# Query and key weights in two halves on two DMA queues, with a new order of instructions

## The chip, the core and the metric

The kernel runs on one core of a Trainium2 chip. The core has five engines with their own instruction queues: TensorE (PE in the profile) does matrix products into PSUM, VectorE (DVE) and ScalarE (ACT) do elementwise work and copy results out of PSUM, GpSimd (POOL) does small work in SBUF, and SyncE (SP) starts transfers between the chip's main memory and SBUF. Sixteen DMA engines carry these transfers, whichever engine started them. Engines wait for each other by semaphores, and each works through its queue in order, so that an instruction that waits holds up everything behind it. The metric is device time in microseconds (us) of one execution; lower is better.

## What is computed

One sequence of 2048 tokens of 448 features, all in bfloat16, goes through an attention block and a mixing block, each with a layer norm before it and a residual after it. The attention has 16 heads of 28 features. Each token attends to eight tokens, itself and those 2, 4, ... 14 positions before it.

```python
h  = x + A(layernorm(x), wqkv, wo)
h2 = h + B(layernorm(h), w_in, w_sp, b_sp, w_out)

# A: q, k, v = x @ wqkv, in 16 heads of 28
idx    = pos[:, None] - 2 * arange(8)[None, :]
logits = einsum('bhsd,bhswd->bhsw', q, k[idx]) * 28 ** -0.5     # masked where idx < 0
o      = einsum('bhsw,bhswd->bhsd', softmax(logits), v[idx])
A      = o @ wo

# B
z      = gelu(x @ w_in)                # 1792 features
z1, z2 = z[:896], layernorm(z[896:])
g      = einsum('ts,bsf->btf', w_sp, z2) + b_sp
B      = (z1 * g) @ w_out
```

## The kernel before

Everything stays in SBUF between the first load and the last store. The tokens are cut into 16 blocks of 128. For each block the kernel computes the mean and variance of x (DVE, lines 677 and 679), the reciprocal root of the variance (POOL, lines 671 and 672), and the normalised block xn (DVE, line 688). The products need xn with features on the partitions, which is called xhT. The first four blocks are transposed on PE by a product with the identity (lines 716 and 719) and copied out of PSUM by the helper `move` (line 576). The other twelve are transposed by DMA.

The weights of q and k are loaded into `wraw`, and DVE and ACT copy them into `wqk`, where each head is padded from 28 to 32 rows. There are eight of these copies, `wp0_0` to `wp3_1`: group g (four heads) and k = 0 for q or 1 for k. A product needs the copies of its own group alone. The products of q and k (`product`, line 565) run over six token ranges `QT`, of which the first two have 128 tokens each. For each range there are four groups, each with eight matmuls into two PSUM banks: six with all 128 rows (features 0 to 383) and two with 64 rows (features 384 to 447), which sit in the upper and lower half of the array. `move` copies the result into `qkT`. Then follow, in 18 pieces of about 112 queries, the logits (line 842, 16 small matmuls), exp (ACT, line 851), the mask (DVE, line 857), the product with v (line 866), the division, a DMA transpose, the product with wo, the residual and the second layer norm. The mixing block follows: w_in, gelu, the second norm, the large product with w_sp (line 1004), the gate (lines 1013 and 1016), the product with w_out (line 1028), the last residual (line 1035) and the stores.

The order is not that of the source. Every piece of work is a `Job` for one engine with the tiles that it reads and writes. `Planner.order` lists the jobs with an assumed duration each, and picks for every engine the ready job that can start, with the lowest rank from the table `PRIO`; `LOOK` says how far ahead an engine may wait for a better-ranked job. `ON` moves single copies to another engine. PSUM banks are tickets that a job takes and another one gives back. The resulting order is then issued with the semaphore waits that the tiles demand. Several names matter below:

- `FIRST` is the order of the first loads, all on SP's queue: x of block 0, the weights of q and k, x of block 1, x of blocks 2 and 3, and so on. The ranks decide the real order among them.
- The job `tbl` on ACT loads the table for exp and runs a small activation that writes two elements of the tile `warm`.
- The filler job, also called warm, is a matmul on constant data that PE does while it has nothing else, until the time `WARMT`. It keeps PE busy at the start. `COLD` is the time until which the planner counts it double.
- `load_c` loads a matrix of 448 rows as one transfer of 384 rows (three to a partition) and two of the last 64 rows, once for each half of the array.

Of the kernel before, what the change touches and what calls it, by code (L numbers as in the profile page):

```python
# [5 lines left out]
S_TOK = 2048  # L6
D = 448
# [5 lines left out]
NB = 16  # L13
# [11 lines left out]
LOOK = {'pe': 0.06465927487231404, 'act': 0.07391855863952959, 'dve': 0.1969035871511503, 'pool': 0.02318129821447599,  # L25
        'sp': 0.10267676699206288}
PRIO = [1, 2, 4, 3, 0, 5, 10, 9, 7, 6, 8, 13, 33, 11, 12, 34, 47, 40, 41, 45, 18, 15, 71, 0, 0, 17, 13, 12, 13, 24, 14,
        23, 27, 22, 25, 28, 26, 0, 3, 11, 14, 16, 7, 8, 11, 9, 6, 15, 3, 16, 12, 1, 16, 5, 18, 29, 17, 12, 17, 20, 17, 23, 15,
        19, 23, 26, 2, 22, 21, 25, 5, 29, 10, 22, 24, 4, 23, 38, 9, 29, 45, 11, 32, 27, 36, 32, 48, 28, 31, 30, 34, 8, 52, 7,
        24, 43, 6, 25, 63, 57, 26, 44, 1, 20, 58, 42, 39, 55, 49, 35, 47, 50, 20, 56, 66, 38, 65, 2, 35, 67, 83, 31, 61, 3, 37,  # L30
        18, 10, 10, 4, 0, 22, 1, 0, 8, 4, 20, 20, 18, 2, 18, 21, 14, 4, 22, 11, 19, 23, 19, 15, 1, 3, 13, 0, 13, 21, 15, 9, 12,
        34, 28, 8, 29, 30, 53, 5, 6, 2, 39, 41, 16, 59, 56, 36, 58, 54, 38, 50, 52, 37, 46, 53, 54, 69, 76, 78, 63, 57, 88, 62,
        71, 42, 42, 51, 89, 102, 96, 109, 92, 95, 56, 91, 103, 65, 89, 86, 48, 24, 27, 7, 10, 24, 35, 6, 46, 49, 51, 40, 21, 30,
        32, 9, 7, 5, 37, 25, 41, 33, 19, 39, 43, 31, 14, 47, 27, 38, 26, 64, 33, 62, 81, 87, 36, 77, 80, 94, 100, 93, 101, 105,
        32, 99, 126, 77, 103, 98, 14, 40, 30, 48, 39, 60, 37, 82, 59, 68, 48, 44, 26, 25, 61, 41, 45, 28, 84, 55, 75, 74, 73,
        27, 83, 85, 104, 122, 116, 107, 96, 33, 69, 34, 75, 97, 31, 19, 64, 40, 36, 43, 86, 81, 85, 79, 72, 43, 70, 67, 34, 60,
        31, 68, 46, 77, 72, 80, 76, 30, 44, 107, 94, 125, 70, 123, 115, 133, 44, 117, 39, 76, 119, 41, 69, 66, 32, 74, 33, 95,
        90, 91, 102, 36, 17, 79, 75, 44, 73, 35, 78, 50, 90, 93, 71, 128, 37, 16, 117, 111, 129, 121, 138, 130, 113, 40, 135,
        110, 82, 162, 43, 85, 88, 29, 87, 47, 92, 104, 131, 127, 35, 73, 84, 82, 49, 65, 45, 97, 67, 114, 110, 118, 132, 38, 74,
        98, 55, 100, 57, 108, 99, 124, 134, 106, 70, 149, 125, 134, 137, 156, 155, 167, 182, 49, 146, 47, 55, 141, 42, 52, 101,  # L40
        105, 60, 116, 63, 133, 64, 147, 129, 136, 153, 46, 54, 77, 118, 53, 108, 66, 112, 139, 145, 154, 45, 49, 171, 152, 143,
        139, 197, 172, 191, 195, 63, 193, 59, 62, 198, 60, 61, 109, 106, 58, 131, 54, 120, 52, 111, 146, 166, 150, 168, 53, 95,
        112, 62, 113, 59, 148, 141, 144, 179, 50, 56, 174, 165, 168, 220, 228, 231, 236, 233, 55, 248, 56, 79, 251, 58, 80, 114,
        115, 120, 122, 76, 127, 78, 151, 136, 170, 142, 48, 63, 241, 121, 70, 147, 72, 176, 153, 192, 199, 61, 64, 107, 206,
# [33 lines left out]
WLH = [4, 4, 8, 9, 18, 1, 4, 12, 24, 4, 14, 34, 6, 22, 21, 26]  # L78
GRES = 1
WARMT = 9.0  # L80
COLD = 7.2
FIRST = [(0, 1), "q", (1, 2), (2, 4), "v", (4, 8), (8, 12), (12, 16), "o"]
LN1G = [(0, 1), (1, 1), (2, 2), (4, 4), (8, 4), (12, 4)]
QT = [(0, 128), (128, 256), (256, 512), (512, 1024), (1024, 1536), (1536, 2048)]
# [120 lines left out]
class Planner:  # L205
# [9 lines left out]
    def job(self, name, eng, key, ops, dur, lat=None, acq=None, rel=None, use=(), after=(), reserve=0, tbl=None, srv=None, kind="F", peer=None):  # L215
        j = Job()
# [884 lines left out]
```

## Time and profile before

| | us |
|---|---|
| median of 3 runs | 244.10 |
| lowest and highest | 244.07, 245.21 |
| the profiled execution's own time | 244.28 |
| its span, first to last instruction | 242.5 |
| PE busy in the span | 234.5 |
| DVE busy | 153.5 |
| ACT busy | 92.3 |
| POOL busy | 40.0 |
| start of the first product with wqk | 8.78 |
| start of the first exp | 14.58 |

The busy time of an engine is a mean over stages with different limits: DVE is close to full until about 110 us and far from it later, and PE is close to full from about 9 us to the end. Matmuls are pipelined, so a matmul's duration in the profile contains its latency; the pace is read from the time that a row of them takes. Times in the text are counted from the start of the span.

### The profile page before, as it was taken

To read this page: it belongs to the slowest core of one execution; us is meant where nothing else is said; L and a number is where in the kernel's file an instruction comes from. 1 tells how busy PE (TensorE), PEld (TensorE's weight loads), DVE (VectorE), ACT (ScalarE), POOL (GpSimd) and SP (SyncE) were. 2 spreads that over 40 slices of the span, in tenths; PEclk is the share of its full clock that TensorE was granted. 3 is DMA by queue.
4 is the path that set the end of the run, shared out by engine and by line. 5 is a ranking of instruction groups with operands and counts; after the bars stand their busy time and mean duration, and the time that the engine had idled before them with its cause. 6 is when DMAs were issued, how large, how long until landed. Compare 5 with 4: busy or idle time off the path is not lost.

```text
span 242.5 us, 4316 instructions
## 1 busy us (share of the span) xinstructions
PE 234.5 (97%) x1735; PEld 114.1 (47%) x1755; DVE 153.5 (63%) x328; ACT 92.3 (38%) x114; POOL 40.0 (16%) x96
## 2 busy tenths in 40 slices
PE   5799999999999999999999999999999999999995
PEld 3565445454545444434444444444444454444453
DVE  4799988999889899999753302602305194416263
ACT  2698768747796998963341000000000000011000
POOL 8346210123232402343111000000000000000000
PEclk9999999999999999999999999999999999999999
DMA  6945565697557878694699950000000002011002
GB/s 186 323 122 103 97 119 120 147 143 178 111 110 105 151 111 171 150 173 118 127 191 167 194 103 0 3 0 0 0 3 1 0 0 78 19 38 38 19 21 95
DMA packets 66468, 23.23 MB, mean 96 GB/s; under 512 B 58896, under 2 KB 66192, under 8 KB 66448
## 3 DMA queue, kind: packets, MB, share of 16 engines
q1 hardware_dynamic: 66448, 22.95, 45.5%
q8 instruction: 14, 0.23, 0.4%
q14 instruction: 6, 0.05, 0.1%
HBM read 6.83 MB, written 1.84 MB: 36 GB/s over the span
## 4 chain that ended last, share of the span: by engine, by line
PE 93%; DMA 2%; DVE 2%; issue 1%; SPq 1%; DVEq 0%
PE psum L1004 40%; PE psum L565 38%; PE psum L1028 9%; PE psum L866 3%; PE psum L842 3%; DMA wraw<-in_A_wqkv_dram 2%; DVE st L677 1%; SPq L591 1%; DVE wqk L576 0%; PE psum L716 0%; DVE srg L1035 0%; DVE xn L688 0%; PE psum L719 0%; DVE mv L679 0%; DVEq L183 0%
## 5 line engine op out<-in xcount | busy, mean ns | idle before, releaser
L1013 DVE TENSOR_TENSOR ub<-psum,bb 128x512 bf16<-128x512 f32 x28 | 19.3, 691 | 53.1 <-PE psum L1004 52.2
L1004 PE MATMUL psum<-wsp_hi,z2p 128*128 128x512 bf16 x220 | 50.6, 379 | 0.2
L971 ACT ACTIVATE z1p<-psum 128x1024 bf16<-128x1024 f32 x14 | 14.0, 1021 | 94.1 <-PE psum L565 94.1
L851 ACT ACTIVATE E<-psum 128x896 bf16<-128x896 f32 (+2 forms) x36 | 31.8, 929 | 8.0 <-PE psum L842 8.0
L1004 PEld LDWEIGHTS psum<-wsp_hi,z2p 128*128 128x128 bf16 x224 | 21.8, 98 | 26.3 <-issue 0.4
L565 PE MATMUL psum<-xhT,wqk 128*128 128x512 bf16 (+5 forms) x186 | 27.8, 306 | 1.8 <-DVE wqk L576 1.2
L1004 PE MATMUL psum<-wsp_la,z2p 128*128 128x512 bf16 x108 | 26.1, 379 | 0.2
L1004 PE MATMUL psum<-wsp_lb,z2p 128*128 128x512 bf16 x110 | 26.0, 379 | 0.1
L565 PE MATMUL psum<-w_in,hnT 128*128 128x448 bf16 (+1 forms) x128 | 25.2, 353 | 0.0
L565 PE MATMUL psum<-hnT,w_in 128*128 128x512 bf16 (+1 forms) x108 | 23.0, 379 | 0.4 <-issue 0.3
L1028 PE MATMUL psum<-w_out,z1p 128*128 128x448 bf16 (+1 forms) x119 | 22.5, 341 | 0.0
L930 DVE BATCH_NORM_STATS2 st<-z2p 128x6 f32<-128x448 bf16 x32 | 19.2, 615 | 4.0 <-ACT z2p L926 3.5
L857 DVE TENSOR_TENSOR E<-E,maskb 128x1792 bf16<-128x1792 bf16 (+2 forms) x18 | 19.6, 1100 | 1.3 <-ACT E L851 1.2
L677 DVE BATCH_NORM_STATS2 st<-x_tm 128x6 f32<-128x448 bf16 x32 | 19.1, 609 | 1.6 <-DMA x_tm<-in_A_x_dram 1.4
L565 PEld LDWEIGHTS psum<-xhT,wqk 128*128 128x128 bf16 (+1 forms) x192 | 13.0, 96 | 12.0 <-issue 2.3
L672 POOL TENSOR_TENSOR rs<-rs,negh 128x2 f32<-128x2 f32 (+2 forms) x22 | 17.6, 801 | 1.8
L1035 DVE TENSOR_TENSOR srg<-psum,x_tm 128x448 bf16<-128x448 f32 (+1 forms) x17 | 10.0, 593 | 11.4 <-PE psum L1028 9.6
L1004 PEld LDWEIGHTS psum<-wsp_lb,z2p 128*128 128x128 bf16 x112 | 10.9, 98 | 13.3 <-issue 0.4
L1004 PEld LDWEIGHTS psum<-wsp_la,z2p 128*128 128x128 bf16 x112 | 11.0, 98 | 13.1
L1028 PEld LDWEIGHTS psum<-w_out,z1p 128*128 128x128 bf16 x119 | 11.6, 98 | 10.2
L565 PEld LDWEIGHTS psum<-w_in,hnT 128*128 128x128 bf16 (+1 forms) x128 | 9.8, 97 | 12.3 <-issue 4.2
L565 PEld LDWEIGHTS psum<-hnT,w_in 128*128 128x128 bf16 (+1 forms) x112 | 9.1, 97 | 11.9 <-issue 2.5
(58 smaller groups left out, 233.9 us busy)
## 6 DMA issues: line engine op xcount, KB each, us to landing
w_in<-in_B_w_in_dram SPq DMA_DIRECT2D x8, 224.0 KB, 3.7
out_dram<-srg SPq DMA_DIRECT2D x16, 112.0 KB, 1.7
x_tm<-in_A_x_dram SPq DMA_DIRECT2D x3, 448.0 KB, 5.9
w_out<-in_B_w_out_dram SPq DMA_DIRECT2D x1, 784.0 KB, 5.3
wraw<-in_A_wqkv_dram SPq DMA_DIRECT2D x1, 672.0 KB, 4.8
bb<-in_B_b_sp_dram SPq DMA_DIRECT2D x1, 512.0 KB, 5.5
wv<-in_A_wqkv_dram SPq DMA_DIRECT2D x1, 336.0 KB, 6.4
wo<-in_A_wo_dram SPq DMA_DIRECT2D x1, 336.0 KB, 6.0
```

Of the source, the lines that this page charges most:

```text
L565: ins = e.matmul(o, w, x, start=g not in seen, stop=left[g] == 0, **kw)
L672: (lambda e: e.tensor_tensor(R, A, negh[:, 0:1].to_broadcast([128, n]), ALU.pow), [rr, r_negh], r_rs[k][m:m + n])],
L677: [(lambda e: e.bn_stats(st[:, m, :], src), [rsrc], [r_st[k][m]])], dve_t(D))
L842: ins = e.matmul(psum[:, c:c + nq], qkT[p:p + DH, 2 * g + 1, k0:k0 + NK], qkT[p:p + DH, 2 * g, t0:t0 + nq], start=True, stop=True, tile_po ...
L851: return e.activation(o, i, AF.Exp, scale=SCALE)
L857: return e.tensor_tensor(a, a, maskb[:, 0:1, pad:pad + nq].to_broadcast([NK, NHEAD, nq]), ALU.mult)
L930: [(lambda e, m=m, k=k: e.bn_stats(st3[:, m, k, :], z2p[:, m, D * k:D * (k + 1)]), [r_z2[m]], [r_st[2][m]])], dve_t(D))
L971: return e.activation(o, i, AF.Gelu_apprx_tanh)
L1004: ins = e.matmul(psv(tk), z2p[:, s, 128 * fc:128 * fc + 128], w[:, 512 * (tc % 2):512 * (tc % 2) + 512], start=(s == 0), stop=(s == NB - 1))
L1013: [(lambda e, tc=tc, s=s, tk=tk: e.tensor_tensor(ub[:, s, :], psv(tk), bb[:, 512 * tc:512 * tc + 512], ALU.add), [r_bb], [r_ub[s]])], dve_ ...
L1028: ins = e.matmul(psv(tk, 0, c1 - c0), z1p[:, fc, 128 * m:128 * m + 128], w_out[:, fc, c0:c1], start=(fc == 0), stop=(fc == FC7 - 1))
L1035: [(lambda e, m=m, s=s, tk=tk, c0=c0, c1=c1: e.tensor_tensor(srg[:, s, c0:c1], psv(tk, 0, c1 - c0), x_tm[:, m, c0:c1], ALU.add), [r_x[m]], ...
```

## The change

Five things are changed in the source, and the ranks, `LOOK` and `ON` are new.

1. The weights of q and k are loaded in two halves. The first half holds groups 0 and 1, the second groups 2 and 3. Each half is four transfers: 384 rows of 224 columns for q, the same for k, and the last 64 rows of both, once for each half of the array. The first half is issued from ACT's queue, the second from SP's. A weight copy waits for its own half alone.
2. The copy of the first block's transpose out of PSUM is cut into two jobs. The transposed block now takes two banks; features 0 to 255 go through DVE, the rest through ACT.
3. The tile warm is set by DVE and not by POOL.
4. A filler job is one matmul and not two, and its stationary operand is a part of the warm tile and not the identity.
5. `COLD` is 6.2 and not 7.2.

By the new ranks, ACT's queue begins with the four transfers, then the table load, the small activation and two weight copies. SP's queue begins with x of blocks 0 and 1, two pieces of the second half, x of blocks 2 to 7, the other two pieces, x of blocks 8 to 11, wv, wo and x of blocks 12 to 15. PE begins with five fillers, the transpose of block 0, four fillers, the transpose of block 1, one filler, 32 matmuls for groups 0 and 1 of the first two token ranges, one filler, 32 for groups 2 and 3, and the transposes of blocks 3 and 2. DVE copies three weight groups where it had four, and ACT five.

```diff
-COLD = 7.2
-FIRST = [(0, 1), "q", (1, 2), (2, 4), "v", (4, 8), (8, 12), (12, 16), "o"]
+XEH = {0: 2}
+COLD = 6.2
+FIRST = [(0, 1), "q0", (1, 2), "q1", (2, 4), "v", (4, 8), (8, 12), (12, 16), "o"]
+QENG = ["act", "sp"]
...
-        r_xh = [spot("xh%d" % m, o_xh, 4 * S_TOK * 2) for m in range(NB)]
+        r_xh = [[spot("xh%d_%d" % (m, i), o_xh, 4 * S_TOK * 2) for i in range(XEH.get(m, 1))] for m in range(NB)]
...
-            elif what == "q":
-                load_c("wq", wraw, A_wqkv[:, 0:2 * D], 2 * D, W_qk, 2.5)
+            elif what[0] == "q":
+                hf, eng = int(what[1]), QENG[int(what[1])]
+
+                def cols(a, hf=hf):
+                    return a.rearrange("p (k n) -> p k n", k=2)[:, :, 224 * hf:224 * hf + 224]
+                for k in range(2):
+                    c0 = D * k + 224 * hf
+                    load("wq%d%d" % (hf, k), lambda c0=c0: wraw[:, 0:3, c0:c0 + 224],
+                         lambda c0=c0: A_wqkv[0:384, c0:c0 + 224].rearrange("(c p) n -> p c n", p=128), [W_qk[hf][k]], 0.5, (1.6, 0.6), eng=eng)
+                for i in range(2):
+                    load("wq%d_%d" % (hf, i), lambda i=i, cols=cols: cols(wraw[64 * i:64 * i + 64, 3, :]),
+                         lambda cols=cols: cols(A_wqkv[384:448, 0:2 * D]), [W_qk[hf][2 + i]], 0.6, (1.6, 0.2), eng=eng)
...
-        pool("warm", -60, [(lambda e: e.memset(warm[:], 1.0), [], [r_warm])], 0.4)
+        pl.job("wset", "dve", -60, [(lambda e: e.memset(warm[:], 1.0), [], [r_warm])], 0.3)
...
-                tk = Ticket(1)
+                nh = XEH.get(m, 1)
+                tk = Ticket(nh)
...
-                move("xe%d" % m, "act", key, lambda m=m: xhT[:, :, 128 * m:128 * m + 128],
-                     lambda tk=tk: psv(tk).rearrange("p (c t) -> p c t", c=4), [], [r_xh[m]], evac_t(512), [tk], tk)
+                for i in range(nh):
+                    lo, hi = 4 * i // nh, 4 * (i + 1) // nh
+                    move("xe%d_%d" % (m, i), ("act", "dve")[i], key, lambda m=m, lo=lo, hi=hi: xhT[:, lo:hi, 128 * m:128 * m + 128],
+                         lambda tk=tk, i=i, lo=lo, hi=hi: psv(tk, i).rearrange("p (c t) -> p c t", c=4)[:, lo:hi], [], [r_xh[m][i]],
+                         evac_t(512 // nh), [tk], (tk, i, 1))
...
-                     W_qk, [r_pad[2 * g + k]], {"act": 0.5, "dve": 0.2})
+                     W_qk[g // 2], [r_pad[2 * g + k]], {"act": 0.5, "dve": 0.2})
...
-        pl.filler = pl.job("warm", "pe", 1e6, [(lambda e: [e.matmul(psv(tkw, 0, 256), ident[:], warm[:, 0:256], start=True, stop=True)
-                                                           for _ in range(2)][-1], [r_ident, r_warm], [])], 0.22, acq=tkw)
+        pl.filler = pl.job("warm", "pe", 1e6, [(lambda e: [e.matmul(psv(tkw, 0, 256), warm[:, 256:384], warm[:, 0:256], start=True, stop=True)
+                                                           for _ in range(1)][-1], [r_warm], [])], 0.11, acq=tkw)
```

The lines of `PRIO`, `LOOK` and `ON`, all of which change, are left out.

## Prediction

> **What bounds the kernel now.** The page's first two parts come first: TensorE (PE) is busy for 97% of the span at full clock, and the only loose slices are the first two. The chain of waits says how the front ends.
>
> ```profile
> span 242.5 us, 4316 instructions
> PE 234.5 (97%) x1735; PEld 114.1 (47%) x1755; DVE 153.5 (63%) x328; ACT 92.3 (38%) x114; POOL 40.0 (16%) x96
> PE   5799999999999999999999999999999999999995
> ...
> 2.78 5.39 DMA wraw<-in_A_wqkv_dram
> ...
> 8.26 0.65 DVE wqk L576 x3
> 8.90 1.68 DVE st L677 x3
> ...
> 12.62 0.39 DVE xn L688
> 13.00 0.05 issue
> 13.05 0.34 PE psum L716 x3
> ```
>
> Columns are start, length, what. The weights of q and k (wraw) land and are released at 8.25; from there to 13.05 the chain runs through VectorE (DVE) to the third and fourth transposes (L716), and then PE never leaves it until 239.84. The windows confirm that:
>
> ```profile
> 8.70:14.00 5.30, 5.10 (x80) 3.90 (x84) 5.30 (x19) 4.43 (x13) 1.32 (x4) 1.00 1.04 324
> 14.00:239.84 225.84, 224.26 (x1629) 107.10 (x1647) 143.98 (x300) 85.37 (x99) 32.39 (x69) 1.00 0.44 86
> ```
>
> Between 14.00 and 239.84 PE idles 225.84 - 224.26 = 1.6 us. The matmuls there are the same in number and shape after the change, so what it can win lies before 14 us, and what it can lose lies anywhere. The timeline of ScalarE (ACT) in the front, then the moved bytes, give the prices:
>
> ```profile
> 8.25 1.51 ACT L576 ACTIVATE wqk<-wraw 128x448 bf16<-128x448 bf16 x3 [1.04 <-DMA wraw<-in_A_wqkv_dram]
> 12.03 1.32 ACT L576 ACTIVATE qkT<-psum 128x256 bf16<-128x256 f32 x4 [0.45 <-PE psum L565]
> 13.61 1.08 ACT L576 ACTIVATE xhT<-psum 128x512 bf16<-128x512 f32 x2 [0.26 <-PE psum L719]
> 14.58 0.93 ACT L851 ACTIVATE E<-psum 128x896 bf16<-128x896 f32 x1
> ...
> 2.00:4.00 2.00, 1.57 (x8) 1.14 (x9) 1.10 (x3) 0.27 (x2) 1.82 (x7) 1.00 0.74 170
> 4.00:6.00 2.00, 1.97 (x13) 0.93 (x11) 1.21 (x5) 0.00 (x0) 1.69 (x6) 1.00 1.09 375
> 6.00:8.00 2.00, 1.54 (x14) 0.98 (x13) 0.58 (x1) 0.60 (x1) 1.41 (x5) 1.00 1.01 287
> 8.00:10.00 2.00, 1.22 (x21) 1.02 (x22) 1.75 (x6) 1.75 (x5) 0.00 (x0) 1.00 1.10 358
> ```
>
> The last two figures are the DMA engines' busy share and GB/s: from 4 us on the engines are full. So earlier weights must come from another order of bytes or from the weak first window (170 GB/s). The first exp (L851) follows the last two block copies (L576, 13.61).
>
> **The change, part by part.** H0 and H1 are the times at which the first and the second half of wraw are released.
>
> *Bytes.* Each half is 2 x 168 + 2 x 56 = 448 KB, all in rows of 448 bytes. On SP's queue now stand x0, x1, two pieces of the second half (224 KB), x2-3 (224), x4-7 (448), then the other two pieces. H1 therefore stands behind 224 + 448 + 448 + 672 = 1792 KB = 1.835 MB, where the old wraw stood behind 1.15 MB. The kernel before had moved 0.34 MB by 4.0, 1.09 by 6.0, 1.66 by 8.0, and 1.835 at 8.5. No row has a 448-byte packet: the trace's DMA packets of 896 bytes take 41 ns and those of 1792 take 74, a line that gives 24.5 at 448 (nearest bounds: 18 ns for the 256-byte ones of the transposes, 41 for 896). I take 24.5, since the line fits both rows that are plain loads. Against 37 ns for half a 1792 this costs 12 ns for each pair; with 1024 x 2 such packets over 16 engines, 64 pairs, 0.77 us, or 0.7 at a busy share of 1.07. From last packet to release the old wraw took 0.3. A second queue can fill part of the weak window: 2 us at 170 where 375 is possible is 1.1 us of loss; I take 0.3 of it back (ends 0 and 0.9). H1 = 8.5 + 0.7 + 0.3 - 0.3 = 9.2.
>
> H0: if the engines take turns row by row between the queues, 64 rows per engine of ACT's pass with 64 of SP's, 1.15 MB: 6.2 + 96 packets x 6 ns (0.55) + 0.3 - 0.3 = 6.8. If ACT's goes first, 0.69 MB is enough: 4.9 + 0.4 + 0.3 = 5.6. I take 6.3, the middle.
>
> The Trainium skill (DMA: Bandwidth & Descriptors, Issuing engines are not separate DMA queues) says that DMAs started by several engines run on the same 16 and that this saves only the sequencer's time; by it H1 would be 9.5 and the gain 0.3 less. The full windows after 4 us agree, the weak first one leaves it open.
>
> *ACT.* Four issues now precede its table load (1.28). SP's rows for issues are 0.40 to 0.59, so 1.6 to 2.4, taken as 2.0: the load and the small activation (0.20) end at 4.3, not 2.28. The warm matmuls wait for that activation, which writes the warm tile; they begin at 4.4, not 2.43. Before, twelve of them took 2.72 us (227 ns each), and eight from 6.50 took 1.05 (131), so PE sped up some 4 us after its start; now that is about 8.5. ACT copies its two of the first half's weights from 6.3 (2 x 0.565), then its half of the first block (0.36, as a 128x256 one at 9.66): the first product can start at 7.8, as DVE's half (below) is done at 7.5. The first half's 32 products then lose at most 0.4 (seven at 114, half of 227, instead of 61 ns), up to 1.7 if all are slow. The wait for H1 covers the small end: 7.8 + 32 x 0.061 + 0.4 = 10.1, while the next weight copy ends at 9.8 and the one that gates the last 16 products at 10.9.
>
> *DVE up to the transposes.* The x path is ready near 5.4 as before (xn of the first block at 4.72 to 5.12, plus about 0.3 because x shares the engines). Then DVE runs in order, from H0: two weight copies 0.45, xn 0.35, half copy 0.38 (half of 0.68 plus its start), three stats 1.65 and an aggregate 0.1, the copy of one qkT 0.38, a weight copy 0.2, three stats 1.6, aggregates 0.4: 5.5 us. That copy of weights waits for H1 with everything behind it: at H0 + 3.3 = 9.6 it doesn't wait while H1 is 9.2. xn starts at 11.8, against 12.60; the transposes run 12.25 to 13.1 (0.87 in the old rows).
>
> *ACT up to exp.* The copies that wait for H1 stand ahead of six evacuations: 9.2 + 3 x 0.565 + 6 x 0.33 = 12.9, against 13.35. Then the two block copies, 1.08, to 14.05, and exp, against 14.58: 0.5 earlier. PE meanwhile does the last 16 products from 10.9 to 11.9 (61 ns each, from 40 in 2.44) and starts the logits at 13.15, against 13.95: 0.8 earlier.
>
> *The rest, at nothing.* SP issues one load more (0.5): it is free from 9.5 to 15.9. POOL loses the warm memset (0.52), and gives the E memset (0.26) a later place: both far from 14.58. DVE's new memset (0.48) and otm's end near 1.9, ahead of x at 2.87. Values of v need wv: H1 + 2.4 for another 784 KB = 11.6, used at 13.5. If those covers went, each would cost its own length at most.
>
> *New order.* Row-tile switches on PE rise by three or four and fall by two; a single one shows as 0.05 to 0.16 in the chain: 0.1 lost. DVE gives three 128x1024 copies to ACT, but neither bounded PE after 14. Bounds: a gain of 1.6 (all idle time gone) and a loss of 2 (a new stall); I take 0.1 lost.
>
> Sum: between 0.5 and 0.8, less 0.1: 0.6. The profiled execution reports 244.28 with a span of 242.5, 0.18 over the median of 244.10. 244.28 - 0.6 = 243.7, and on the median's footing 243.5. Its own range: H1 from 8.5 to 9.8, 242.8 to 244.1.
>
> **Rivals.**
>
> 1. *Two queues fill the weak start.* H0 5.5, H1 8.4: ACT 8.4 + 1.7 + 2.0 + 1.1 = 13.2 at exp (1.4 earlier), logits at 12.35 (1.6 earlier): 1.5, so 242.6. For it: 0.74 busy share until 4.0. Against: the first wraw packets took 0.4 to 0.9 us each on half the engines, with nothing else to blame.
>
> 2. *Two late engines again.* In the DMA records the last wraw piece lands on 14 engines by 7.6 and on two at 8.2 and 8.5. If these two lag by 1.0 in the new order also, H1 is 10.2, exp at 15.0: 0.4 lost, 244.5. For it: the lag lasts until 14 us. Against: one packet of 1444 and one of 984 ns made it, and they need not come back.
>
> 3. *Short rows cost as much as long ones; slower.* At 41 ns a 448-byte packet adds 128 x 16.5 / 1.07 = 2.0 to H1: 11.2, exp at 16.0, logits at 15.0: 1.05 to 1.4 lost, 245.4. It decides from about 30 ns on (H1 9.8, no gain), and passes 0.5% near 39. For it: nothing in this trace is a plain load under 512 bytes. Against: the line through 41 and 74. The Trainium skill (DMA: Bandwidth & Descriptors, Specifications) asks at least 512 B for line rate, with read-modify-write below; at twice 24.5 by its rule H1 would be 12.2 and the time 246.4, an estimate.
>
> 4. *PE stays slow through the front.* Warm matmuls stop near 6.8 for want of the second block, and all 32 products run at 114 ns: done at 11.4, the other 32 at 13.4, the transposes (0.87) at 14.2, logits 0.25 later than before: 244.3, the change then doing nothing. For it: PE waits for the second xn, behind DVE's weight copies. Against: before, PE sped up across two waits of 0.2.
>
> 5. *A stall in the dense stretch by the new order*, 2 us: 245.5. Against: 1.6 us of idle time in all before.
>
> **Chances.** Forecast 0.34, rival one 0.27, two 0.10, three 0.14, four 0.05, five 0.10. What a measurement of this kernel can tell from no change is about 0.5%, 1.2 us. Faster: rival one and 0.06 of the forecast, 0.33. Slower: five and 0.12 of three, 0.22. Same: the rest, 0.45. The range runs from 242.1 (rival one with its end of 0.9 in place of 0.3 taken back in full) to 245.9 (rivals three and five with 0.4 of spread over them), with about 0.15 outside.
>
> **What would show it.** First matmul with wqk near 7.8 (8.78 before); ACT's copies of the second half from 9.2; xn of blocks 2 and 3 at 11.8; exp at 14.05; packets of 448 bytes at 24.5 ns; PE idle after 14 still near 1.6. Wrong if H1 is past 9.8, if the first 32 products take over 3 us, or if PE's idle after 14 grows by over 1.

## The result: 1.1% slower

| | before | after |
|---|---|---|
| median, us | 244.10 | 247.27 |
| lowest and highest of 7 runs each | 243.16, 245.54 | 246.12, 247.49 |
| profiled execution, us | 244.28 | 247.49 |
| its span | 242.5 | 245.8 |
| first product with wqk | 8.78 | 10.30 |
| logits start | 13.95 | 16.87 |
| PE's last matmul ends | 239.84 | 242.36 |

The ratio is 1.0106, with a 95% interval of 1.0072 to 1.014. The forecast was 243.5 with a range to 245.9. The profiled execution is the slowest of its seven. The changed kernel's page first:

```profile
span 245.8 us, 4303 instructions
PE 234.1 (95%) x1720; PEld 114.3 (46%) x1742; DVE 151.3 (62%) x323; ACT 96.1 (39%) x120; POOL 39.9 (16%) x96
PE   1799999999999999999999999999999999999994
```

PE is busy as long as before, and the first slice has fallen from 5 to 1. Pieces of its chain of waits and its timeline say what happened there (start, length, engine, instruction; in brackets the idle time before it and what ended that):

```profile
0.80 0.74 ACTq L598
2.22 0.65 ACTq L598
2.90 5.54 DMA wraw<-in_A_wqkv_dram
10.37 3.44 PE psum L572 x32
14.02 2.12 PE psum L572 x32
```

```profile
0.80 2.71 ACTq L598 DMA_DIRECT2D wraw<-in_A_wqkv_dram  x4
4.84 0.20 ACT L680 ACTIVATE warm<-warm 1x2 bf16<-1x2 bf16 x1
5.10 1.25 PE L1064 MATMUL psum<-warm 128*128 128x256 bf16 x5 [5.10 <-ACT warm L680]
6.85 1.03 PE L1064 MATMUL psum<-warm 128*128 128x256 bf16 x4
8.46 0.47 DVE L583 COPY wqk<-wraw 128x448 bf16<-128x448 bf16 x2 [3.29 <-DMA wraw<-in_A_wqkv_dram]
8.84 0.40 DVE L705 TENSOR_SCALAR xn<-x_tm,mv,rs 128x448 bf16<-128x448 bf16 x1
9.29 0.50 PE L735 MATMUL psum<-ident,xn 128*128 128x128 bf16 x3 [1.41 <-DVE xn L705]
10.30 3.51 PE L572 MATMUL psum<-xhT,wqk 64*128 64x128 bf16 x32
11.77 1.50 ACT L583 ACTIVATE wqk<-wraw 128x448 bf16<-128x448 bf16 x3
13.81 2.33 PE L572 MATMUL psum<-xhT,wqk 128*128 128x128 bf16 x32
15.98 0.33 PE L735 MATMUL psum<-ident,xn 128*128 128x128 bf16 x3
16.87 0.40 PE L863 MATMUL psum<-qkT 28*128 28x128 bf16 x16
```

The same products in the timeline before:

```profile
8.78 1.56 PE L565 MATMUL psum<-xhT,wqk 128*128 128x128 bf16 x24 [1.23 <-DVE wqk L576]
10.48 2.44 PE L565 MATMUL psum<-xhT,wqk 64*128 64x128 bf16 x40
```

Four issues on ACT's queue take 2.71 us, so that the warm matmuls begin at 5.10. The first half of the weights is released at 8.46, later than the whole was before (8.25). The second block's xn stands behind weight copies on DVE, and PE waits 1.41 for it. Then 32 products take 3.51 us, 110 ns each, where 24 took 1.56 before, 65 each.

The end is 3.3 us later in three parts: logits 16.87 - 13.95 = 2.92 late; from there to PE's last matmul 225.49 against 225.89, 0.40 shorter; after it 3.44 against 2.66, 0.78 longer. Of the 2.92, 10.30 - 8.78 = 1.52 is a later first product; from there to the third transpose it is 5.68 against 4.27, 1.41 more. The end, first the chain and then the timeline:

```profile
236.84 5.52 PE psum L1049 x36
242.36 0.61 DVE srg L1056
242.98 0.30 DVEq L1088
243.27 0.30 DVE srg L1056
```

```profile
241.82 1.75 DVE L1056 TENSOR_TENSOR srg<-psum,x_tm 128x448 bf16<-128x448 f32 x4 [1.67 <-DMA out_dram<-srg]
```

By the new ranks block 12's residual follows block 8's closely, and both use the same store buffer: DVE waits 1.67 us for that store, which took 2.84 us to land.

### The profile page after: what moved, and what is told of

It reads as the page before. It is cut to its first block, busy times and chain, and to the rows that moved or that the text cites. A ratio compares the mean times of both kernels' runs of the same rounds, so it can differ in the third digit from the quotient of the medians.

```text
span 245.8 us, 4303 instructions
## 1 busy us (share of the span) xinstructions
PE 234.1 (95%) x1720; PEld 114.3 (46%) x1742; DVE 151.3 (62%) x323; ACT 96.1 (39%) x120; POOL 39.9 (16%) x96
## 3 DMA queue, kind: packets, MB, share of 16 engines
HBM read 6.83 MB, written 1.84 MB: 35 GB/s over the span
## 4 chain that ended last, share of the span: by engine, by line
PE 87%; DVE 6%; DMA 2%; POOL 2%; issue 1%; ACTq 1%; DVEq 0%
PE psum L1025 39%; PE psum L572 33%; PE psum L1049 9%; DMA wraw<-in_A_wqkv_dram 2%; PE psum L887 2%; PE psum L863 2%; DVE st L694 1%; DVE x_tm L831 1%; POOL rs L689 1%; DVE E L878 1%; ACTq L598 1%; DVE otm L898 1%; DVE xn L705 1%; POOL rs L688 1%; DVE mv L696 0%
## 5 line engine op out<-in xcount | busy, mean ns | idle before, releaser
L992 ACT ACTIVATE z1p<-psum 128x1024 bf16<-128x1024 f32 x14 | 13.8, 1023 | 94.6 <-PE psum L572 94.6
L572 PE MATMUL psum<-xhT,wqk 128*128 128x512 bf16 (+5 forms) x185 | 29.3, 323 | 0.6 <-issue 0.3
L1025 PE MATMUL psum<-wsp_la,z2p 128*128 128x512 bf16 x109 | 25.6, 379 | 0.2
L572 PEld LDWEIGHTS psum<-xhT,wqk 128*128 128x128 bf16 (+1 forms) x192 | 14.3, 104 | 11.7 <-issue 2.8
L1037 DVE TENSOR_TENSOR z1p<-ub,z1p 128x512 bf16<-128x512 bf16 x28 | 11.8, 424 | 11.0 <-ACT z1p L992 10.2
L689 POOL TENSOR_TENSOR rs<-rs,negh 128x2 f32<-128x2 f32 (+2 forms) x22 | 18.1, 824 | 1.8
L688 POOL TENSOR_SCALAR rs<-mv 128x2 f32<-128x2 f32 (+2 forms) x22 | 8.2, 374 | 56.0 <-DVE mv L696 32.2
L583 ACT ACTIVATE qkT<-psum 128x1024 bf16<-128x1024 f32 (+2 forms) x20 | 14.3, 738 | 6.4 <-PE psum L572 6.2
```

What stands on the lines that cost most here:

```text
L572: ins = e.matmul(o, w, x, start=g not in seen, stop=left[g] == 0, **kw)
L583: j = pl.job(name, eng, key, [(lambda e: e.activation(o(), i(), AF.Copy) if eng == "act" else e.tensor_copy(o(), i()), list(reads), list(w ...
L689: (lambda e: e.tensor_tensor(R, A, negh[:, 0:1].to_broadcast([128, n]), ALU.pow), [rr, r_negh], r_rs[k][m:m + n])],
L992: return e.activation(o, i, AF.Gelu_apprx_tanh)
L1025: ins = e.matmul(psv(tk), z2p[:, s, 128 * fc:128 * fc + 128], w[:, 512 * (tc % 2):512 * (tc % 2) + 512], start=(s == 0), stop=(s == NB - 1))
L1037: [(lambda e, fc=fc, tc=tc, s=s: e.tensor_tensor(z1p[:, fc, 512 * tc:512 * tc + 512], ub[:, s, :], z1p[:, fc, 512 * tc:512 * tc + 512], AL ...
```

## The experiments

Two theories stood against each other. The first: PE works at half pace through the 64 products, since the warm-up begins late, is short and has a gap, and DVE's queue has x behind the weights. The second: the split loading itself, with its short rows, two queues and eight issues, brings the weights too late. Where no other kernel is named, an edit is made to the changed kernel, and ratios are to the kernel before on the same chip.

**Seven warm matmuls more**, which fill the 1.4 us ahead of the second transpose.

```diff
+        at = [i for i, j in enumerate(ordered) if j.name == "xT1"][0]
+        ordered[at:at] = [[j for j in ordered[:at] if j.name == "warm"][-1]] * 7
```

> The changed kernel with 7 more warm matmuls between the first two transposes, which fill the 1.4 us in which PE stood idle; they still wait for ACT and begin at 5.10. Theory A (the late start alone keeps PE slow): PE is busy from 5.10 on and reaches full pace only some 3.5 to 4.5 us later, near 9.0, so the products from 10.3 are fast: about 2.0 us for the first 32, logits near 15.3, 245. Theory A2 (PE changes its pace only after a longer stretch, or at fixed moments): part of the first 32 is slow, 246. Theory B (the pace depends on something other than PE's own activity): no change, 3.5 us for the first 32.

Measured 244.94 us (10 runs), ratio 1.0045 (1.0027 to 1.0063). From its timeline:

```profile
6.85 2.09 PE L1064 MATMUL psum<-warm 128*128 128x256 bf16 x11
8.39 0.46 DVE L583 COPY wqk<-wraw 128x448 bf16<-128x448 bf16 x2 [3.21 <-DMA wraw<-in_A_wqkv_dram]
9.90 2.06 PE L572 MATMUL psum<-xhT,wqk 64*128 64x128 bf16 x32
14.96 0.40 PE L863 MATMUL psum<-qkT 28*128 28x128 bf16 x16
```

Nothing else is changed, the weights come when they came, and the logits start 1.91 earlier. Work that computes nothing made the kernel faster: the interval of the ratio lies clear of the changed kernel's. Of the 2.92 us, 1.01 are left.

**Whole weights again**, from SP's queue as before, all else as changed.

```diff
+        for n, i in (("wq00", -1), ("wq0_1", 1), ("wq0_0", 0)):    # whole rows: 384, then twice the last 64
...
+            w0[n].eng, w0[n].ops = "sp", [(f, [], wr, True)]
+        at = [i for i, j in enumerate(ordered) if j.name == "x1"][0] + 1
+        ordered[at:at] = [w0["wq00"], w0["wq0_1"], w0["wq0_0"]]
```

> The changed kernel with the loading of the weights undone: three transfers of whole rows from SyncE's queue behind x of blocks 0 and 1, as before; all else (warm tile from VectorE, one warm matmul at a time, half copies, ranks) as changed. Theory A (the warm-up with its gap and the order on VectorE cost the time, whatever loads the weights): warm matmuls from 2.3 but again only nine of them, weights released at 8.25, the second block's normalisation behind the weight copies at 8.7, first product at about 10.0 and 32 of them in over 3.2 us, logits at 16.2 to 16.8, 246.3 to 247.2. Rival B (the split loading from two queues costs the time): logits at 14.0 to 14.5, 243.8 to 244.6.

Measured 247.12, ratio 1.013 (1.0096 to 1.0165): undoing the headline of the change gives nothing back. The warm-up now starts at 2.34, but has a gap of 1.54 in it, and PE then waits 2.51 for the second xn:

```profile
2.34 1.25 PE L1064 MATMUL psum<-warm 128*128 128x256 bf16 x5 [2.34 <-ACT warm L680]
8.53 0.46 DVE L583 COPY wqk<-wraw 128x448 bf16<-128x448 bf16 x2 [3.46 <-DMA wraw<-in_A_wqkv_dram]
9.36 0.50 PE L735 MATMUL psum<-ident,xn 128*128 128x128 bf16 x3 [2.51 <-DVE xn L705]
10.36 3.51 PE L572 MATMUL psum<-xhT,wqk 64*128 64x128 bf16 x32
```

**Warm-up from an own tile**: the table's small activation gets a tile of its own, so that warm matmuls start at 1.54, and 18 more are issued.

```diff
+            if j.name == "tbl":
+                j.ops = [(lambda e: e.activation(tblt[0:1, 0:2], tblt[0:1, 0:2], AF.Exp), [r_tblt], [r_tblt])]
...
+        for name, n in (("xT0", 10), ("xT1", 8)):
+            at = [i for i, j in enumerate(ordered) if j.name == name][0]
+            ordered[at:at] = [[j for j in ordered[:at] if j.name == "warm"][-1]] * n
```

> The changed kernel with a tile of its own for ACT's small activation, so that the warm matmuls no longer wait for ACT, and 18 more of them; the loads stay as they are. Theory A (the slow clock of PE costs the front 1.5 us): the first 32 products take about 2.0 us instead of 3.51, the logits start near 15.3, about 245.8. Theory B (PE's pace is hidden behind the late second half and the stats): the products are fast, and the logits move by under 0.4; 247.

Measured 244.98, ratio 1.006 (1.0039 to 1.0081). (The lines that make and set the new tile are left out.) The first half is released at 8.7, and the products are fast, though PE waited 2.37 us just before:

```profile
9.51 0.34 PE L737 MATMUL psum<-ident,xn 128*128 128x128 bf16 x3 [2.37 <-DVE xn L707]
10.19 2.06 PE L574 MATMUL psum<-xhT,wqk 64*128 64x128 bf16 x32
```

**x ahead of the weights** on DVE and ACT, nothing else.

```diff
+        names = ("xe0_0", "xe0_1", "xe1_0", "wp0_0", "wp0_1", "wp1_0", "wp1_1")
+        moved = [[j for j in ordered if j.name == n][0] for n in names]
+        first = [j for j in ordered if j.name in ("xT1", "n0_1")]
...
+        ordered[at:at] = sorted(first, key=lambda j: j.name) + moved
```

> The changed kernel with the second block's xn and the block copies of the first two blocks ahead of the four weight copies of the first half on VectorE and ACT. Theory A (work on x queued behind a wait for weights): the second transpose moves from 9.29 to about 6.9, the first product from 10.30 to about 9.1, the logits by 1.2 to 15.7; about 246.1. Theory B (the pace of a cold PE and the second half set the front): the first product moves, the logits do so by under 0.4; 247.

Measured 247.31, ratio 1.0158 (1.0132 to 1.0184). The products begin 0.6 earlier, and now both batches are slow, so the logits start at 17.64:

```profile
9.70 0.29 PE L572 MATMUL psum<-xhT,wqk 64*128 64x128 bf16 x2 [0.92 <-ACT wqk L583]
10.17 3.40 PE L572 MATMUL psum<-xhT,wqk 64*128 64x128 bf16 x30 [0.17 <-ACT wqk L583]
13.58 3.34 PE L572 MATMUL psum<-xhT,wqk 128*128 128x128 bf16 x32
```

**First half on SP's queue**, behind x of blocks 0 and 1.

```diff
+        for j in [j for j in ordered if j.name.startswith("wq0")]:
+            ordered.remove(j)
+            j.eng = "sp"
+            ordered.insert([i for i, k in enumerate(ordered) if k.name == "x1"][0] + 1, j)
```

> The changed kernel with the first half of the weights issued from SP's queue too, right behind x of blocks 0 and 1; nothing else moves. Theory A (ACT's queue is what held the first half: its rows take turns with SP's, and its issues hold up the table load and with it the warm matmuls): the first half is released near 6.0 instead of 8.46, warm matmuls start near 2.5 instead of 5.10, the first product near 7.5 instead of 10.30, the logits near 14.2 instead of 16.86; 2.5 us faster than the changed kernel, about 244.8. Theory B (rows of 448 bytes and the DMA engines hold it, whichever queue): the first half stays past 7.5 and under 1 us is won.

Measured 245.91, ratio 1.0089 (1.006 to 1.0118). The first half comes 2 us earlier, at 6.50, and the products begin at 8.38. They take 3.19 and PE then waits for the second half (copied at 11.79), so the logits start at 15.52. One queue brought the half earlier than two.

**The kernel before, two edits**: its three weight transfers at the head of ACT's queue, and its warm matmuls left out.

```diff
...
+            j.eng = "act"                # j: wq, wq_0, wq_1
+        ordered[0:0] = wq
```

> The kernel before with its three weight loads (rows of 1792 bytes) moved from SP's queue to the head of ACT's; nothing else. Theory A (the move of loads to ACT's queue is what costs, by the table load and the warm matmuls behind it): three issues of 0.43 to 0.68 put the table load at 2.5 or later, the warm matmuls begin near 4.1 instead of 2.43, and the products run at half pace for part of the front; the weights land within 0.5 of 8.25; logits 0.5 to 1.5 later than 13.95, 0.5 to 1.5 us slower. Theory B (a second queue fills the idle start of the DMA engines): the weights are released before 7.5 and the kernel is as fast or faster.

```diff
+        ordered = [j for j in ordered if j is not pl.filler and j.name != "warm" or j.eng != "pe"]
```

> The kernel before without its 24 warm matmuls; nothing else moves. It prices PE's slow pace by itself, with the weights where they were. Theory A (a PE that was not kept busy runs the products of the front at half pace): the 64 products from 8.8 take over 6 us instead of 4.1, the transposes of blocks 2 and 3 start near 15.5 instead of 13.05, and the time rises by 2 us or more. Theory B (the front is bound by the copies and the stats): 0.5 us or less.

The first measured 245.7, ratio 1.0071 (1.0044 to 1.0098): the table load starts at 2.48 and the warm-up at 4.13. The weights land no later than before (7.84 against 8.17), but x of block 1, now beside them, is there at 6.27 (3.63 before), ACT copies the weights at 9.92 (8.25 before), and 24 products take 2.19:

```profile
7.46 0.50 PE L716 MATMUL psum<-ident,xn 128*128 128x128 bf16 x3 [0.61 <-DVE xn L688]
10.99 2.19 PE L565 MATMUL psum<-xhT,wqk 128*128 128x128 bf16 x24
```

The second measured 246.05, ratio 1.007 (1.0044 to 1.0096). The medians lie 2.2 us apart, as its first theory had it, though the 64 products took 5.39 us and not over 6; the profile is that of the fastest of seven executions, 244.7. So the warm-up before is worth 0.4 to 1.0%, and ACT's queue costs about as much even without halves, by late x as well as by the late warm-up. The first kernel's ten times fall into two groups, 244.64 to 245.07 and 246.33 to 247.03; the profile is one of the slower group.

**The kernel before with halves from SP's queue** (eight issues where it had three, rows of 448 bytes).

```diff
+            if j.name == "wq":
+                j.ops = half(0) + half(1)
...
+            elif j.name[:2] == "wp" and j.name[2].isdigit():
+                j.ops = [(j.ops[0][0], r_h2[int(j.name[2]) // 2], j.ops[0][2])]
```

> The kernel before, with the weights of q and k loaded by four transfers of each half in place of three of the whole, all still from SyncE's queue and in the old place; rows of 448 bytes in place of 896, nothing else changed. Theory A (short rows cost by their bytes, as the 24 to 28 ns of each 448-byte packet in the changed kernel's trace say): the first half is released by about 7.2, the whole by 8.3 to 8.9 (three more issues on SyncE before x of blocks 4 to 7), copies of the first half start earlier but the copies of x's transpose stand before them, so products start at 8.6 to 9.0 and the time is 244.0 within 0.5 of before. Theory B (short rows cost as much as long ones): whole weights released at 9.5 or later, products at 10 or later, 245.0 to 245.6.

Measured 245.76, ratio 1.0068 (1.0047 to 1.009). Both theories of it missed: the halves came early (copies at 6.60 and 8.74), as the first had it, but the time is that of the second. The loss is in x of the next blocks, whose issue moved from 3.41 to 6.59; DVE waits for them twice (0.44 and 0.80), and xn of blocks 2 and 3 runs at 14.07 where it was 12.60:

```profile
6.59 1.11 SPq L591 DMA_DIRECT2D x_tm<-in_A_x_dram  x2
9.47 1.15 DVE L677 BATCH_NORM_STATS2 st<-x_tm 128x6 f32<-128x448 bf16 x2 [0.44 <-DMA x_tm<-in_A_x_dram]
14.07 0.70 DVE L688 TENSOR_SCALAR xn<-x_tm,mv,rs 128x448 bf16<-128x448 bf16 x2
```

**Store buffers of blocks 12 and 15 exchanged.**

```diff
-                s = m % NS
+                s = {12: 3, 15: 0}.get(m, m % NS)
```

> The changed kernel with the store buffers of blocks 12 and 15 exchanged; order and work are the same. Theory A (at the end the last residual of block 12 waits 1.67 us for the store of block 8, which was issued just before from the same buffer): that wait goes and the end comes 0.8 us earlier, about 246.5. Theory B (the end is bound by PE's last products and the landing of the last store): no change, 247.3.

Measured 246.47, ratio 1.0111 (1.0082 to 1.0141), which can't be told from the changed kernel's 1.0106. The wait is gone in the trace (the last residual ends 0.4 us after PE), but in the runs with own tile and with the gap filled it is down to 0.48 without this edit and no longer reaches the end: the store before it took 1.66 us to land there, and 2.84 in the changed kernel.

**Attempts at the best of both**: both halves on SP's queue behind x0 and x1, wv ahead of x of blocks 8 to 11, own tile with 24 warm matmuls, x first, buffers exchanged, statistics of blocks 4 to 7 later; then also those of blocks 2 and 3 behind the second half's copies; then also x0 and x1 from ACT's queue.

```diff
+        for j in after("x1", ["wq00", "wq0_0", "wq01", "wq0_1", "wq10", "wq1_0", "wq11", "wq1_1"]):
+            j.eng = "sp"
...
+        after("n0_2", ["st0_4", "st0_5", "st0_6", "st0_7", "mv0_4", "mv0_5", "mv0_6", "mv0_7", "rs0_4"])
...
+        after("wp2_1", ["st0_2", "mv0_2", "st0_3", "mv0_3", "rs0_2"])                 # second attempt
...
+            if j.name in ("x0", "x1"):                                                  # third
+                j.eng = "act"
```

> The changed kernel with all its weights on SP's queue, both halves right behind x of blocks 0 and 1, wv ahead of x of blocks 8 to 11; the table's activation on a tile of its own and more warm matmuls; x's work ahead of the waits for weights; stats of blocks 4 to 7 behind xn of blocks 2 and 3; store buffers of blocks 12 and 15 exchanged. Theory A (the front was lost to the late first half, the order behind it and the slow PE, and the new order of the rest is sound): first products near 7.2, xn of blocks 2 and 3 near 11, logits near 12.5 instead of 13.95 of the kernel before; 1 to 2 us faster than the kernel before, about 242.5. Theory B (the rest of the new order depends on the late front, or x of blocks 2 to 7 comes too late behind the weights): no faster than before, 244 or more.

> The changed kernel with both halves of the weights on SyncE's queue behind x of blocks 0 and 1, the warm-up from a tile of its own and without a gap, the block copies of x ahead of the weight copies, the two last store buffers exchanged, and now the statistics of blocks 2 and 3 behind the copies of the second half. Theory A (what cost the changed kernel its time is TensorE's slow pace after an idle gap, and work queued on VectorE behind data that comes late): first products at about 8.3, all 64 done by 12.4 without a gap over 0.5 us, logits at 13.4 to 13.9, time 0.2 to 0.8 below before. Rival B (the second half itself lands at 10 or later): a gap of about 1.5 us remains between the two batches of products, logits at 14.5 or later, time 0.5 to 2 above before.

> As the run with the statistics moved back, and x of blocks 0 and 1 issued from ScalarE's queue, so that SyncE's queue begins with the weights. Theory A (two queues fill the weak start, each first row earlier): first half released at about 6.0, second at 8.0 to 8.5, logits at 12.5 to 13.0, time about 1 below before. Rival B (the two queues share each engine row by row, and the bytes ahead of the first half are the same): first half released at 6.5 to 7.2, and x of block 0 later than 3.5, logits at 13.4 or later, time no better than without this move.

Measured 247.26 (ratio 1.0136, 1.0109 to 1.0163), 247.2 (1.012, 1.0085 to 1.0154) and 247.39 (1.0119, 1.0059 to 1.0178): all missed. In the first, statistics that wait 2.65 us for x of block 2 stand ahead of a weight copy on DVE; PE waits 1.79 and is slow afterwards. The second removes that: products at 7.79 and 10.40, logits at 14.24, still 0.29 after the kernel before. But the statistics put off come due later, and a copy of qkT on DVE is late:

```profile
22.22 1.04 PE L574 MATMUL psum<-xhT,wqk 128*128 128x256 bf16 x8 [1.79 <-DVE qkT L585]
```

The third has its products later (8.88 and 11.57), the first 32 of them slow (2.74 us), and the same wait.

**The rest of the change, repaired**: whole weights, own tile with 24 warm matmuls in place of ten, x first, buffers exchanged (the edits above together). And **the same with the changed loading left in**, which differs from it by the loading alone.

> As the run with whole weights, and with the warm-up from a tile of its own without a gap, the block copies and the second block's normalisation ahead of the weight copies, and the two last store buffers exchanged. Theory A (with these the rest of the change is neither better nor worse than before): weights 8.25, products at 8.8 to 9.3 with 32 in 2.1 us, xn of blocks 2 and 3 at 12.6 to 12.8, logits at 13.9 to 14.2, 244.0 within 0.6 of before. Rival B (the new ranks hold a gain of their own in the dense stretch that the slow front hid; TensorE idled 0.16 us there in two runs against 1.6 before): 0.8 or more below before.

> The repaired kernel with whole weights once more, for a narrower interval, and beside the split loading. Theory A: 0 to 0.6 us under before, ratio 0.9975 to 1.000. Rival B (the lower time of its first runs was this chip's): 0.3 or more above before.

> The repaired kernel (warm-up from a tile of its own without a gap, block copies and second normalisation ahead of the weight copies, last store buffers exchanged) with the changed loading left in: first half from ScalarE's queue, second from SyncE's. It differs from the repaired kernel with whole weights by the loading alone. Theory A (the changed loading itself brings the first half later than the whole weights came before, 7.6 to 8.7 in the runs so far against 7.3 to 8.5): first half 7.8 to 8.5, first products at 9.0 to 9.7 and 32 of them in 2.1 us, second half 10.4, xn of blocks 2 and 3 at 12.5 to 13.0, logits at 14.0 to 14.6, 0.4 to 1.2 slower than with whole weights. Rival B (the loading costs nothing once the rest is repaired): within 0.3 of it.

With whole weights: 243.4, ratio 0.9992 (0.9966 to 1.0018), and again, 243.77, 0.9999 (0.9981 to 1.0018): the kernel before, within what can be told (one of ten and one of twelve executions lie higher, at 245.74 and 245.43). With the changed loading, beside the second of these: 244.68, ratio 1.0041 (1.0015 to 1.0067), with logits 1.6 later than was expected in the profiled execution. Whole weights in the first of these profiles:

```profile
7.30 0.78 DVE L585 COPY wqk<-wraw 128x448 bf16<-128x448 bf16 x2 [0.97 <-DMA wraw<-in_A_wqkv_dram]
8.48 2.00 PE L574 MATMUL psum<-xhT,wqk 64*128 64x128 bf16 x30 [0.23 <-ACT wqk L585]
10.44 2.16 PE L574 MATMUL psum<-xhT,wqk 128*128 128x128 bf16 x32
```

The changed loading, then its window from 9.3 to 13.8 (PE, PEld, DVE, ACT and POOL busy, granted clock, DMA share, GB/s):

```profile
8.73 0.46 DVE L585 COPY wqk<-wraw 128x448 bf16<-128x448 bf16 x2 [2.13 <-DMA wraw<-in_A_wqkv_dram]
9.45 0.23 PE L574 MATMUL psum<-xhT,wqk 64*128 64x128 bf16 x2 [1.34 <-ACT wqk L585]
9.92 2.75 PE L574 MATMUL psum<-xhT,wqk 64*128 64x128 bf16 x30 [0.23 <-ACT wqk L585]
12.68 2.78 PE L574 MATMUL psum<-xhT,wqk 128*128 128x128 bf16 x32
```

```profile
9.30:13.80 4.50, 4.11 (x44) 3.14 (x45) 4.46 (x16) 2.64 (x7) 1.12 (x3) 0.66 1.11 298
```

This profile is one in which PE lost its pace: 92 ns for each of 30 products, at a granted clock of 0.66. (The trace's clock records have full clock from 7.36 to 10.77, half to 14.19, and full clock again.) The eleven times of this kernel fall into two groups, six from 243.44 to 244.68 and five from 245.80 to 246.32. I read the two groups as PE's two paces; only one execution has a profile, so that is argued. The lower group's middle, 244.1, lies 0.4 over the median with whole weights. So the loading costs a few tenths by its lateness, and in five of eleven some 1.9 us more.

**The gap filled and x first.** Sixteen warm matmuls more ahead of the first product, on top of x first.

```diff
+        at = [i for i, j in enumerate(ordered) if j.name == "qk0_0H"][0]
+        ordered[at:at] = [[j for j in ordered[:at] if j.name == "warm"][-1]] * 16
```

> The changed kernel with sixteen warm matmuls more ahead of the first products, and with the block copies and the second block's normalisation ahead of the weight copies; loading as changed. Theory A (what the filled gap left of the loss is VectorE's work of 0.8 us queued behind the first half): products at 9.5 with 32 in 2.1 us, xn of blocks 2 and 3 at 12.9 to 13.3, logits at 14.2 to 14.6, 0.3 to 0.8 faster than with the gap filled alone, 0.1 to 0.6 above before. Rival B (the second half, landing at 10.4, sets the end in any case): logits at 14.9 or later, ratio as with the gap filled alone.

Measured 245.65, ratio 1.0077 (1.0055 to 1.0099). This run doesn't answer its question: the 17 warm matmuls from 8.36 on ended at 10.87, after the weight copies (10.0), and put the products off to 10.80. They were fast then (2.06).

PE's pace in all profiles, in one table. "Wait" is PE's longest idle time between its first matmul and the first batch of products; the pace is the row's time over its number. "Full clock from" is where the trace's first record of the granted clock begins; three profiles hold none.

| kernel | warm-up starts | warm matmuls ahead | wait | ns each product | full clock from | logits |
|---|---|---|---|---|---|---|
| before | 2.43 | 22 | 1.23 | 65 (24) | 5.40 | 13.95 |
| changed | 5.10 | 10 | 1.41 | 110 (32) | 14.16 | 16.87 |
| x first | 5.10 | 10 | 0.92 | 113 (30) | 16.44 | 17.64 |
| buffers exchanged | 5.10 | 10 | 0.72 | 110 (32) | no record | 16.71 |
| whole weights | 2.34 | 10 | 2.51 | 110 (32) | 15.42 | 17.40 |
| first half on SP | 2.34 | 10 | 1.59 | 100 (32) | 10.99 | 15.52 |
| gap filled | 5.10 | 17 | 0.28 | 64 (32) | 8.36 | 14.96 |
| x first, 16 more | 5.08 | 26 | none | 64 (32) | 9.38 | 15.68 |
| own tile | 1.54 | 28 | 2.37 | 64 (32) | 4.57 | 15.25 |
| first attempt | 1.54 | 24 | 0.42 | 64 (32) | 6.70 | 16.05 |
| second attempt | 1.54 | 24 | 0.55 | 64 (32) | no record | 14.24 |
| third attempt | 1.54 | 24 | 0.56 | 86 (32) | 10.46 | 15.26 |
| repaired, whole | 1.54 | 24 | 0.73 | 67 (30) | no record | 13.55 |
| the same again | 1.54 | 24 | 0.85 | 67 (30) | 6.69 | 13.99 |
| repaired, split | 1.54 | 24 | 1.34 | 92 (30) | 7.36 | 16.19 |
| before, halves | 2.43 | 22 | none | 72 (10) | 6.70 | 15.42 |
| before, ACT's queue | 4.13 | 22 | 0.61 | 91 (24) | 12.53 | 16.51 |
| before, no warm-up | none | 0 | 1.65 | 84 (64) | 11.93 | 14.58 |

Ten warm matmuls leave the products slow wherever they stand. Of the twelve profiles with 17 or more, nine have fast products, and their number and the longest wait don't tell which: own tile is fast after 2.37, the third attempt is slow after 0.56 and the kernel before with ACT's queue after 0.61.

The clock records say more. Their lengths are whole multiples of 3.41 us (3.41, 6.83, 232.11). Counted back from the first record in steps of 3.41, each of the 15 profiles that have records came to full clock behind a step in which PE was busy for 0.86 or more of the time. Ahead of that, no step of 0.84 or less brought it, and one of 0.92 (x first) didn't either. In the changed kernel the two steps ahead of the products' own have 0.66 and 0.59; with the gap filled the step that ends at 8.36 has 0.95. The steps lie differently in each execution: with the warm-up at 1.54, full clock came at 4.57, 6.69, 6.70, 7.36 or 10.46.

## Why the prediction was wrong

**The step that failed** is "The first half's 32 products then lose at most 0.4 ..., up to 1.7 if all are slow. The wait for H1 covers the small end". All were slow: 3.51 us, 1.45 more than the 2.06 of the fast runs, and no wait covered it, since PE itself ended the chain: ACT came to the second half's copies at 11.77, and the half had landed at 10.72. With the slow transposes the pace is worth 1.91 of the 2.92 us by which the logits are late, as the run with the gap filled shows. The prediction put the speed-up at about 8.5 by counting some 4 us from the first warm matmul, whatever PE did in them. The runs show that it must be busy: with the same start at 5.10, seven more matmuls make the same products fast. A second step failed beside it, H0, below; the 1.01 that are left I put down to it and to the order on DVE. Of the three signs of being wrong that the prediction gave, two came: H1 past 9.8, and the first 32 products over 3 us.

The Trainium skill (TensorE: Matmul & The Clock Gate, Part 1) has PE at half clock until about 3.4 us of sustained activity, judged in a window that runs free of the program, so that the turn differs from run to run. The traces agree: 110 ns against 64, and clock records in multiples of 3.41 us. Two kernels' times in two groups would fit it, but each has a profile of one execution only.

**Rival four**, PE slow through the front, was the right mechanism, at a chance of 0.05 and a price of 244.3. What it had against it, that PE before sped up across waits of 0.2, was no evidence for a wait of 1.41. Its price let the slow products run from 7.8, beneath the wait for the second half; they ran from 10.30.

**H0** was forecast at 6.3 (5.6 to 6.8) and came at 8.46, 7.6 to 8.7 in the runs with this loading. The two queues take turns, as the end of 6.8 had it: by 6.0 ACT's had moved 798 packets of data and SP's 715. But the bytes by then were taken from the kernel before, 1.09 MB, and were 0.81. Between 4 and 6 us, where the kernel before had 375 GB/s, the changed kernel, the run with the first half on SP's queue and the kernel before with ACT's queue had:

```profile
4.00:6.00 2.00, 0.90 (x5) 0.66 (x6) 1.11 (x3) 1.03 (x2) 1.62 (x5) 1.00 0.84 185
4.00:6.00 2.00, 0.82 (x6) 0.49 (x7) 0.80 (x3) 0.00 (x0) 1.69 (x6) 1.00 0.73 156
4.00:6.00 2.00, 1.87 (x10) 1.31 (x10) 0.45 (x2) 0.00 (x0) 0.81 (x2) 1.00 1.08 341
```

So the low rate goes with the halves and not with the second queue: halves from one queue moved 0.72 MB by 6.0 (0.76 in the kernel before with halves), whole weights on a queue of their own 1.16. Two things could hold it, and no run parts them. In the DMA records single packets of 448 bytes took up to 1.16 us there. And the small pieces are slow to issue: with the first half on SP's queue, six of them with 0.69 MB took 3.78 us, which would be 180 GB/s, an estimate from these rows.

**Rival one** put H0 at 5.5 and H1 at 8.4; the changed kernel had moved more by 4.0 (0.45 MB against 0.34), but less by 6.0, so it is wrong. The Trainium skill's rule that issuing engines are not separate DMA queues (DMA: Bandwidth & Descriptors) has the right sign, but the 9.5 for H1 that was worked out from it was early too.

**H1**, forecast 9.2, landed at 10.72 (9.97 to 11.09 in the runs with this loading), past the stated limit of 9.8 and past the 10.2 of rival two; but the last piece came in engine by engine from 8.72 on and not with two engines behind the rest. From its last packet to its release it took 0.72, where 0.3 was taken; the trace of the kernel before has 0.6 for this, and has its last piece in on 14 engines by 7.32 and on two at 7.94 and 8.17, each some 0.3 earlier than the prediction read.

**DVE's queue.** The working put the weight copies at H0 ahead of the second xn and priced only their length. With H0 at 8.46 the xn, the second transpose and both block copies came after it. Of the 1.52 by which the first product is late, x first alone took 0.60 away; what is left I put down to the late half and ACT's copies of it, which no run shows by itself.

**The issues on ACT** took 2.71 where 2.0 was taken (0.68 each, SP's rows had 0.40 to 0.59), and moved the warm-up to 5.10, not 4.4. It is the piece and not the engine that costs: SP's issues of the same pieces took 0.59 to 0.74, and three issues of whole weights took 1.66 on either.

**The end.** A wait for a store was in no rival. It cost 0.78 in the profiled execution and is not regular: where the store landed in 1.66 us, it cost nothing.

**What was right.** Packets of 448 bytes took 25 ns in nine of ten records, 24.5 by the line through the longer ones, so rival three falls. The Trainium skill (DMA: Bandwidth & Descriptors, Specifications) asks at least 512 bytes for line rate, and the prediction estimated 246.4 from it at twice the packet's time; these loads don't bear that out, with 25 ns against 41 for 896 bytes. The dense stretch has no new stall, so rival five falls:

```profile
14.00:243.00 229.00, 226.66 (x1668) 109.18 (x1687) 143.13 (x302) 90.68 (x109) 33.05 (x71) 1.00 0.43 85
```

Of the 2.3 us of idle time here 0.64 lie behind PE's last matmul; 1.7 are left, where the kernel before had 1.6, and from the logits to PE's end the kernel is 0.40 shorter. That the new ranks hold a gain of their own is not borne out: the repaired kernel has them and is level.

## What to carry to other kernels

At the start of a kernel, look at how long one matmul takes before asking when its data comes: a row of 128-column products at 110 ns is PE at half pace, and a few matmuls on constant data, without a gap until the real ones, can be worth more than earlier weights. Transfers at the head of a compute engine's queue, here 0.68 us each, put off all that stands behind them, and a load cut into pieces is issued as many times. When a copy may wait for late data, see that nothing which is ready stands behind it on its engine.

## What the runs showed of the hardware

- The granted clock in a window does not show the slow start, since the records begin with the first full clock and what lies ahead of them counts as 1.00. The changed kernel, whose records begin at 14.16, has 1.00 from 9.3 to 13.8 with products at 110 ns; the split repaired one has 0.66 with 92.

```profile
9.30:13.80 4.50, 4.50 (x39) 3.33 (x40) 3.70 (x11) 3.17 (x8) 0.80 (x2) 1.00 1.11 309
```

- How long an idle time PE forgives is not fixed by its length: 2.37 us after 28 warm matmuls kept the pace, 1.34 after 24 lost it in the profiled execution, and 1.79 in the first of the attempts. While PE is still slow, 0.56 and 0.61 were enough to put full clock off to 10.46 and 12.53.
- Loads of the weights in halves moved fewer bytes in the first 6 us than whole ones, whether by one queue (0.72 and 0.76 MB against 1.09) or two (0.81 against 1.16), and the first half came at 8.46 from a queue of its own, 6.50 from the queue that it shared.
